# Decode attention with a gated SwiGLU mix: V's loads move from SP's DMA queue to ACT's

## The chip, the cores and the metric

The kernel runs on one core of a Trainium2 chip. The metric is the device time of one execution in microseconds (us); lower is better. "The profile" is one execution recorded by the hardware profiler, with its page and its trace; L187 is line 187 of the kernel before.

## The reference

One new token (batch 1, width 512) goes through two branches, and a sigmoid gate mixes them. Branch A is attention over a cache of 65,536 keys in each of 32 heads, head width 128; branch B is a small SwiGLU.

```python
def _A_ref(x, k_cache, v_cache, wq, wo):          # x: 1 x 1 x 512
    q = (x @ wq).reshape(B, Sq, 32, 128).transpose(0, 2, 1, 3)
    scores = einsum("bhqd,bhkd->bhqk", q, k_cache) * 128 ** -0.5
    p = softmax(scores)                           # 65536 keys in each head
    o = einsum("bhqk,bhkd->bhqd", p, v_cache)
    return o.transpose(0, 2, 1, 3).reshape(B, Sq, 4096) @ wo
def _B_ref(x, w_gate, w_up, w_down):              # 512 -> 1792 -> 512
    return (silu(x @ w_gate) * (x @ w_up)) @ w_down
g = sigmoid((x * gate_w).sum(-1))
return g * A + (1 - g) * B
```

All tensors are bfloat16. The K and V caches are 512 MiB each, and every byte of them is read once.

## The kernel before

It is written in Bass: every engine has an instruction list of its own, and the lists meet only in semaphores. Each head is cut into 8 chunks of 8192 keys (`NCH`, `CK`), so there are 256 K chunks and 256 V chunks (`NT`). A chunk is 2 MiB: 128 partitions with 16 KiB each. In this text k7 is K chunk 7, v7 is V chunk 7, and head h owns chunks 8h to 8h+7 of either kind.

All chunks pass through one ring of 7 buffers (`ring`, `NS`). The order in which they take buffers is `ring_order`: k0 to k9 first, then k10, v0, k11, v1 and so on, V trailing K by `LAG` = 10 chunks, and v246 to v255 at the end. Chunk number n of that list uses buffer n % 7, and its load may start when chunk n-7 has been used. Because 7 is odd and the kinds alternate, the load of a V chunk waits for a K chunk to have been transposed (`ktdone`), and the load of a K chunk waits for a V chunk to have been multiplied (`pvdone`): the load of v(j) waits for the transpose of k(j+7), and that of k(j+14) for the use of v(j). Only among the last ten, where V follows V, is it partly otherwise.

The work on the chunks:

- DVE transposes each K chunk into `kt` (two buffers, L269). After the first chunk of the next head is transposed, it takes the row maximum of the finished head's scores (`mxs`, L275).
- TensorE multiplies the transposed K chunk by the query into `psS` (L346, 64 matmuls), and in the same step the V chunk ten behind by the probabilities into `psO` (L363, 64 matmuls).
- GpSimd reduces the maximum over the partitions (`amx`, L201) and scales it into the bias (`nbias`, L203); later it sums the exponentials (`Lt`, L205).
- ACT does one exponential over the scores of each head (`pa`, L217), as soon as the bias is there. It has hardly anything else to do: two small exponentials at the start (L210, L212), and the store of the output at the end (L220).
- DVE rearranges `pa` into `pb` (L285, 16 copies), which TensorE needs before the head's first V chunk, and normalises a head's result (L290, L292). TensorE adds each head's part of the output product (L372).

SP issues every load, in program order: the two small rows, `wq`, k0 and k1, the three SwiGLU weights, then the chunks in `ring_order`, with `wo` ahead of number 12. Where SP waits for a buffer, all later loads wait behind it.

Of the kernel before, what the change touches and what calls it, by code (L numbers as in the profile page):

```python
# [9 lines left out]
NS = 7  # L10
# [3 lines left out]
ACT = mybir.ActivationFunctionType  # L14
# [8 lines left out]
def bass_gated_mix__mha_block_cached__swiglu_ffn__decode_kernel(  # L23
# [11 lines left out]
    out: bass.AP,  # L35
):
    _, H, S, Dh = A_k_cache.shape
    D = A_wq.shape[0]
    F = B_w_gate.shape[1]
    Dc = D // P  # L40
    FC = F // P
    NCH = S // CK
    NT = H * NCH
    SCALE = float(Dh) ** -0.5
    assert Dh == 128 and D == 512 and F % P == 0 and NCH * RB == 512

    ring_order = []
# [6 lines left out]
    slot = {}  # L54
# [5 lines left out]
    with ExitStack() as ctx:  # L60
        def sb(name, shape, dt):
            return ctx.enter_context(nc.sbuf_tensor(name, shape, dt))

        def psum(name, shape, dt):
            return ctx.enter_context(nc.psum_tensor(name, shape, dt))

        def sem(name):
            return ctx.enter_context(nc.semaphore(name))

        psS = psum("psS", [P, 2, 512], F32)  # L70
# [21 lines left out]
        nbias = sb("nbias", [P, H], F32)  # L92
        rsum = sb("rsum", [P, H], F32)
# [3 lines left out]
        pa = sb("pa", [P, 2, 512], BF16)  # L97
        pb = sb("pb", [P, 2, 512], BF16)
        ring = sb("ring", [P, NS, RB * Dh], BF16)
# [5 lines left out]
        rs = [sem(f"rs{i}") for i in range(NS)]  # L105
# [16 lines left out]
        ktdone = sem("ktdone")  # L122
        qkdone = sem("qkdone")
        pvdone = sem("pvdone")
        s_mx = sem("s_mx")
        s_ar = sem("s_ar")
        s_nb = sem("s_nb")
        expdone = sem("expdone")
        s_pb = sem("s_pb")
# [15 lines left out]
        def kv_src(kind, j):  # L145
            src = A_k_cache if kind == "k" else A_v_cache
            h, c = j // NCH, j % NCH
            return src[0, h, c * CK:(c + 1) * CK, :].rearrange("(p r) d -> p (r d)", p=P)
# [18 lines left out]
        MLP_AT = 2  # L167
        WO_AT = 12

        @block.sync  # L170
        def _(sp):
            sp.dma_start(xrow[0:1, :], xr_dram).then_inc(s_x, 16)
            sp.dma_start(gwrow[0:1, :], gw_dram).then_inc(s_x, 16)
            sp.dma_start(wq_t[:], wq_dram).then_inc(s_wq, 16)
            for n, (kind, j) in enumerate(ring_order):
                if n == MLP_AT:
                    sp.dma_start(wg_t[:], wg_dram).then_inc(s_w1, 16)
                    sp.dma_start(wu_t[:], wu_dram).then_inc(s_w1, 16)  # L178
                    sp.dma_start(wd_t[:], wd_dram).then_inc(s_w1, 16)  # L179
                if n == WO_AT:  # L180
                    sp.wait_ge(s_b, 1)
                    sp.dma_start(wo_t[:], wo_dram).then_inc(s_wo, 16)
                if n >= NS:
                    pkind, pj = ring_order[n - NS]
                    sp.wait_ge(ktdone if pkind == "k" else pvdone, pj + 1)
                sl = slot[(kind, j)]
                sp.dma_start(ring[:, sl, :], kv_src(kind, j)).then_inc(rs[sl], 16)  # L187

        @block.gpsimd
        def _(pool):  # L190
# [16 lines left out]
        @block.scalar  # L207
        def _(act):
            act.wait_ge(s_z, 1)
            nc.scalar.activation(sc[0:1, 1:2], sc[0:1, 0:1], ACT.Exp, scale=-1.0).then_inc(s_e1, 1)  # L210
            act.wait_ge(s_h, 1)
            nc.scalar.activation(hbuf[:, 0, 0:FC], psM[:, 64:64 + FC], ACT.Exp, scale=-1.0).then_inc(s_sig, 1)  # L212
            for h in range(H):
                act.wait_ge(s_nb, h + 1)
                if h >= 2:
                    act.wait_ge(s_pb, h - 1)
                nc.scalar.activation(pa[:, h % 2, :], psS[:, h % 2, :], ACT.Exp, bias=nbias[:, h:h + 1],  # L217
                                     scale=SCALE, accum_out=rsum[:, h:h + 1]).then_inc(expdone, 1)
            act.wait_ge(s_fin, 1)
            act.dma_start(out_dram, fin[0:1, :]).then_inc(s_out, 16)  # L220
            act.wait_ge(s_out, 16)
# [182 lines left out]
```

## Time and profile before

| | |
|---|---|
| median of 3 runs | 2604.34 us (2604.3 to 2604.63) |
| the profiled execution: its own time | 2604.43 us |
| the profiled execution: its span | 2602.6 us |
| busy: DVE, TensorE matmul, ACT, GpSimd | 1324.6, 946.4, 26.6, 34.7 us |
| HBM read | 1087.64 MB, 418 GB/s over the span |
| granted TensorE clock | 1.0 at first, 0.5 from the second of 40 slices on |

The span runs from the first to the last instruction recorded on the core; 1.8 us of the profiled execution's time lie outside it. "DMA" is the mean busy share of the core's 16 DMA engines, which carry the packets of all queues. q1 is the queue of SP, q10 that of ACT, q8 fetches instructions. "SPq" and "ACTq" rows are DMA instructions issued by these engines. Idle time is put down to what ended it.

### The profile page before, as it was taken

The numbers are of one execution on the slowest core, as the hardware profiler recorded it, in microseconds if no ns is written. First come the engines' busy times: TensorE is split into PE (matmuls) and PEld (weight loads), VectorE is DVE, ScalarE is ACT, GpSimd is POOL, SyncE is SP. The second block draws the span as 40 slices with busy tenths as digits, with TensorE's granted clock in tenths as the row PEclk, the third lists the DMA queues.
The fourth block names the chain that finished last, engine by engine and source line by source line (L and its number), as shares of the span: only waits on it lengthen the run. The fifth ranks groups of instructions, "written<-read, shape, count | busy, mean of one in ns | idle before, by whom it ended". The sixth has DMA issues, their size and how long they took to land.

```text
span 2602.6 us, 68273 instructions
## 1 busy us (share of the span) xinstructions
PE 946.4 (36%) x33062; PEld 906.0 (35%) x33062; DVE 1324.6 (51%) x883; ACT 26.6 (1%) x67; POOL 34.7 (1%) x105
## 2 busy tenths in 40 slices
PE   2333333333333333333333333333333333333334
PEld 2333333333333333333333333333333333333333
DVE  4655454554455554555545555455555454554451
ACT  0000000000000000000000000000000000000000
POOL 0000000000000000000000000000000000000000
PEclk9555555555555555555555555555555555555555
DMA  9999999999999999999999999999999999999997
GB/s 397 412 426 426 426 425 426 426 426 427 425 426 426 425 425 427 425 423 419 426 421 423 420 421 423 425 421 420 421 420 425 422 420 425 415 426 423 420 420 309
DMA packets 81512, 1092.03 MB, mean 420 GB/s; under 512 B 8275, under 2 KB 14166, under 8 KB 15190
## 3 DMA queue, kind: packets, MB, share of 16 engines
q1 hardware_dynamic: 81236, 1087.67, 99.1%
q8 instruction: 258, 4.23, 0.7%
q14 instruction: 16, 0.13, 0.0%
q10 hardware_dynamic: 2, 0.00, 0.0%
HBM read 1087.64 MB, written 0.00 MB: 418 GB/s over the span
## 4 chain that ended last, share of the span: by engine, by line
DMA 76%; DVE 12%; PE 9%; issue 1%; SPq 1%; ACT 0%; POOL 0%; POOLq 0%; DVEq 0%
DMA ring<-in_A_k_cache_dram 75%; DVE kt L269 11%; PE psS L346 5%; PE psO L363 4%; DMA ring<-in_A_v_cache_dram 1%; SPq L179 1%; SPq L187 0%; DVE pb L285 0%; PE psB L331 0%; PE psM L324 0%; SPq L178 0%; ACT pa L217 0%; DVE mxs L275 0%; DVE brow L260 0%; POOL amx L201 0%
## 5 line engine op out<-in xcount | busy, mean ns | idle before, releaser
L269 DVE STREAM_TRANSPOSE kt<-ring 128x4096 uint32<-128x4096 uint32 x256 | 1137.5, 4445 | 1142.6 <-DMA ring<-in_A_k_cache_dram 1141.5
L346 PE MATMUL psS<-qd,kt 128*128 128x4 bf16 x16384 | 478.2, 166 | 1606.3 <-DVE kt L269 1606.3
L346 PEld LDWEIGHTS psS<-qd,kt 128*128 128x128 bf16 x16384 | 457.0, 104 | 1640.6 <-DVE kt L269 1640.6
L363 PE MATMUL psO<-pb,ring 128*128 128x1 bf16 x16384 | 472.8, 165 | 30.8 <-DMA ring<-in_A_v_cache_dram 22.7
L363 PEld LDWEIGHTS psO<-pb,ring 128*128 128x128 bf16 x16384 | 456.8, 104 | 32.2 <-DMA ring<-in_A_v_cache_dram 23.8
L285 DVE COPY pb<-pa 32x128 bf16<-32x128 bf16 x512 | 154.5, 302 | 71.3 <-ACT pa L217 64.7
L217 ACT ACTIVATE pa<-psS,nbias 128x512 bf16<-128x512 f32 x32 | 22.0, 687 | 2475.1 <-POOL nbias L203 2475.1
L201 POOL PARTITION_ALL_REDUCE amx<-mxs x32 | 11.8, 368 | 1945.2 <-DVE mxs L275 1945.2
L292 DVE TENSOR_SCALAR oTn<-psO,Li 128x1 bf16<-128x1 f32 x32 | 7.1, 222 | 30.1 <-PE psO L363 29.1
L275 DVE TENSOR_REDUCE mxs<-psS 128x1 f32<-128x512 f32 x32 | 20.9, 653 | 2.0 <-PE psS L346 2.0
L372 PE MATMUL psY<-wo_t,oTn 128*1 128x512 bf16 x32 | 18.8, 587 | 0.4 <-DVE oTn L292 0.4
L205 POOL PARTITION_ALL_REDUCE Lt<-rsum x32 | 12.8, 400 | 285.6 <-issue 285.6
L203 POOL TENSOR_SCALAR nbias<-amx 128x1 f32<-128x1 f32 x32 | 8.3, 260 | 294.4 <-issue 294.4
L310 PE MATMUL psM<-xTb,wq_t 128*128 128x1 bf16 x128 | 3.5, 165 | 11.5 <-DMA wq_t<-in_A_wq_dram 11.5
L310 PEld LDWEIGHTS psM<-xTb,wq_t 128*128 128x128 bf16 x128 | 3.5, 104 | 11.6 <-issue 11.6
L245 DVE CAST qTb<-psM 128x32 bf16<-128x32 f32 x1 | 0.2, 192 | 14.0 <-PE psM L310 14.0
L217 ACT ACTIVATION_READ_ACCUMULATOR pa<-psS,nbias 128x1 f32 x32 | 6.2, 193 | 0.0
L290 DVE RECIPROCAL Li<-Lt 128x1 f32<-128x1 f32 x32 | 4.0, 123 | 3.9 <-POOL Lt L205 3.9
L331 PE MATMUL psB<-wd_t,guT 128*1 128x512 bf16 x14 | 5.9, 613 | 0.0
L260 DVE TENSOR_SCALAR brow<-psB,sc 1x512 f32<-1x512 f32 x1 | 0.7, 737 | 6.5 <-PE psB L331 6.5
L324 PE MATMUL psM<-xTb,wu_t 128*128 128x1 bf16 x56 | 3.2, 165 | 2.1 <-issue 2.1
L324 PEld LDWEIGHTS psM<-xTb,wu_t 128*128 128x128 bf16 x56 | 2.7, 104 | 2.1 <-issue 2.1
(31 smaller groups left out, 19.3 us busy)
## 6 DMA issues: line engine op xcount, KB each, us to landing
ring<-in_A_k_cache_dram SPq DMA_DIRECT2D x256, 2048.0 KB, 31.2
ring<-in_A_v_cache_dram SPq DMA_DIRECT2D x256, 2048.0 KB, 29.9
wq_t<-in_A_wq_dram SPq DMA_DIRECT2D x1, 4096.0 KB, 12.7
wo_t<-in_A_wo_dram SPq DMA_DIRECT2D x1, 4096.0 KB, 32.0
wg_t<-in_B_w_gate_dram SPq DMA_DIRECT2D x1, 1792.0 KB, 26.5
wu_t<-in_B_w_up_dram SPq DMA_DIRECT2D x1, 1792.0 KB, 30.3
wd_t<-in_B_w_down_dram SPq DMA_DIRECT2D x1, 1792.0 KB, 33.8
xrow<-in_A_x_dram SPq DMA_DIRECT2D x1, 1.0 KB
```

The source lines that it names most:

```text
L179: sp.dma_start(wd_t[:], wd_dram).then_inc(s_w1, 16)
L201: nc.gpsimd.partition_all_reduce(amx[:, h:h + 1], mxs[:, h:h + 1], P, RMAX).then_inc(s_ar, 1)
L203: nc.gpsimd.tensor_scalar_mul(nbias[:, h:h + 1], amx[:, h:h + 1], -SCALE).then_inc(s_nb, 1)
L205: nc.gpsimd.partition_all_reduce(Lt[:, h:h + 1], rsum[:, h:h + 1], P, RADD).then_inc(s_L, 1)
L217: nc.scalar.activation(pa[:, h % 2, :], psS[:, h % 2, :], ACT.Exp, bias=nbias[:, h:h + 1], scale=SCALE, accum_out=rsum[:, h:h + 1]).then_i ...
L269: nc.vector.transpose(o, src).then_inc(ktdone, 1)
L275: nc.vector.reduce_max(mxs[:, h:h + 1], psS[:, h % 2, :], AX_X).then_inc(s_mx, 1)
L285: last = nc.vector.tensor_copy(dst, sr)
L292: nc.vector.tensor_scalar(oTn[:, h:h + 1], psO[:, h % 2, h:h + 1], Li[:, h:h + 1], None, ALU.mult).then_inc(s_otn, 1)
L346: last = nc.tensor.matmul(psS[:, h % 2, col:col + 4], ktb[i % 2][:, je // 2, r, :, je % 2], qd[:, h, je, :], start=(je == 0), stop=(je == 3))
L363: last = nc.tensor.matmul(psO[:, h % 2, h:h + 1], ring[:, slot[("v", v)], r * Dh:(r + 1) * Dh], pb[:, h % 2, c * RB + r:c * RB + r + 1], s ...
L372: last = nc.tensor.matmul(psY[0:1, :], oTn[:, h:h + 1], wo_t[:, h, :], start=(h == 0), stop=(h == H - 1))
```

## The change

V's loads are taken out of SP's list and put into ACT's. SP keeps everything else: the small rows, all weights, and K's loads. The conditions on which a load may start, the buffers and `ring_order` stay as they are; a new helper `load` holds the wait and the DMA for both engines.

On ACT the loads stand in program order with the exponentials: the load of v(8h), then the exponential of head h with its waits (`s_nb`, `s_pb`), then the loads of v(8h+1) to v(8h+8), then the exponential of head h+1. All of them stand behind the SwiGLU's exponential (L212 before). ACT's DMA instructions go to ACT's own queue.

```diff
+        def load(eng, n):
+            kind, j = ring_order[n]
+            if n >= NS:
+                pkind, pj = ring_order[n - NS]
+                eng.wait_ge(ktdone if pkind == "k" else pvdone, pj + 1)
+            sl = slot[(kind, j)]
+            eng.dma_start(ring[:, sl, :], kv_src(kind, j)).then_inc(rs[sl], 16)
+
         @block.sync
         def _(sp):
...
-                if n >= NS:
-                    pkind, pj = ring_order[n - NS]
-                    sp.wait_ge(ktdone if pkind == "k" else pvdone, pj + 1)
-                sl = slot[(kind, j)]
-                sp.dma_start(ring[:, sl, :], kv_src(kind, j)).then_inc(rs[sl], 16)
+                if kind == "k":
+                    load(sp, n)
...
-            for h in range(H):
-                act.wait_ge(s_nb, h + 1)
-                if h >= 2:
-                    act.wait_ge(s_pb, h - 1)
-                nc.scalar.activation(pa[:, h % 2, :], psS[:, h % 2, :], ACT.Exp, bias=nbias[:, h:h + 1],
-                                     scale=SCALE, accum_out=rsum[:, h:h + 1]).then_inc(expdone, 1)
+            for n, (kind, j) in enumerate(ring_order):
+                if kind != "v":
+                    continue
+                load(act, n)
+                if j % NCH == 0:
+                    h = j // NCH
+                    act.wait_ge(s_nb, h + 1)
+                    if h >= 2:
+                        act.wait_ge(s_pb, h - 1)
+                    nc.scalar.activation(pa[:, h % 2, :], psS[:, h % 2, :], ACT.Exp, bias=nbias[:, h:h + 1],
+                                         scale=SCALE, accum_out=rsum[:, h:h + 1]).then_inc(expdone, 1)
```

## Prediction, made before the change was run

> **What bounds the kernel now.** I read the page's slices and queues first, then the issues, then the timeline in the middle and at the end.
>
> ```profile
> DMA  9999999999999999999999999999999999999997
> GB/s 397 412 426 426 426 425 426 426 426 427 425 426 426 425 425 427 425 423 419 426 421 423 420 421 423 425 421 420 421 420 425 422 420 425 415 426 423 420 420 309
> ...
> q1 hardware_dynamic: 81236, 1087.67, 99.1%
> q8 instruction: 258, 4.23, 0.7%
> ...
> q10 hardware_dynamic: 2, 0.00, 0.0%
> ```
>
> The 16 DMA engines are busy from the second slice to the last but one, at about 426 GB/s for the first 1100 us and about 421 afterwards. All of it is SP's queue, q1. No engine is near its limit (DVE has the largest share, 51%). So the time is bytes over rate: 1092 MB at the page's mean of 420 GB/s are 2600 us of a 2602.6 us span. The bytes do not change. The time can change only if DMA engines stand idle, or if they move bytes at another rate.
>
> ```profile
> ring<-in_A_k_cache_dram SPq DMA_DIRECT2D x256, 2048.0 KB, 31.2
> ring<-in_A_v_cache_dram SPq DMA_DIRECT2D x256, 2048.0 KB, 29.9
> ```
>
> A load lands some 30 us after its issue. In the timeline K chunks come every 9.8 us (transposes at 1024.37, 1034.15, 1043.94), so one load takes 4.9 us of all engines, and 30 / 4.9 = 6 loads are in the queue at any time. That is the cover that a late issue has.
>
> ```profile
> 1034.15 4.45 DVE L269 STREAM_TRANSPOSE kt<-ring 128x4096 uint32<-128x4096 uint32 x1 [5.34 <-DMA ring<-in_A_k_cache_dram]
> 1038.52 0.65 DVE L275 TENSOR_REDUCE mxs<-psS 128x1 f32<-128x512 f32 x1
> 1038.62 0.33 SPq L187 DMA_DIRECT2D ring<-in_A_v_cache_dram  x1
> ...
> 1039.27 0.37 POOL L201 PARTITION_ALL_REDUCE amx<-mxs  x1 [62.89 <-DVE mxs L275]
> ...
> 1042.26 0.33 SPq L187 DMA_DIRECT2D ring<-in_A_k_cache_dram  x1
> ...
> 1048.42 0.33 SPq L187 DMA_DIRECT2D ring<-in_A_v_cache_dram  x1
> ...
> 1048.56 0.26 POOL L203 TENSOR_SCALAR nbias<-amx 128x1 f32<-128x1 f32 x1 [8.92 <-issue]
> 1048.85 0.69 ACT L217 ACTIVATE pa<-psS,nbias 128x512 bf16<-128x512 f32 x1 [80.17 <-POOL nbias L203]
> ```
>
> This is a head's turn, and the place where the new order of ACT's list bites. The transpose of k(8h+8) frees the buffer for v(8h+1), issued at 1038.62. The same transpose lets DVE take the head's maximum, and the exponential comes only after GpSimd, at 1048.85: between the row of its reduction, 0.37 us, and that of the bias lie 8.92 us.
>
> ```profile
> 2530.55 37.57 SPq L187 DMA_DIRECT2D ring<-in_A_v_cache_dram  x8
> ...
> 2542.22 4.45 DVE L269 STREAM_TRANSPOSE kt<-ring 128x4096 uint32<-128x4096 uint32 x1 [5.35 <-DMA ring<-in_A_k_cache_dram]
> ...
> 2560.02 0.69 ACT L217 ACTIVATE pa<-psS,nbias 128x512 bf16<-128x512 f32 x1 [69.97 <-POOL nbias L203]
> ...
> 2597.43 1.86 PE L363 MATMUL psO<-pb,ring 128*128 128x1 bf16 x64 [3.01 <-DMA ring<-in_A_v_cache_dram]
> ```
>
> The end: k255 lands at 2542.2, its head's exponential runs from 2560.02, the last V chunk lands at 2597.4, and 5 us of small work follow. The V loads of this stretch are issued ahead of that exponential.
>
> **The change, part by part.** *Issuing.* 256 DMA instructions of 0.33 us (84 us) leave SP and come to ACT; ACT's one DMA of before, the output, took 0.50 us, so 84 to 128 us. SP was idle in waits for most of the span, ACT is busy 1%. ACT's exponential of head h stands behind the load of v(8h), which is free once k(8h+7) is transposed, one K period (9.8 us) before the maximum is even taken. Both ends cost nothing: 0 us. That ACT issues on a queue other than SP's shows in q10, the output's.
>
> *K's loads* no longer stand behind V's waits. But they were issued on release already (1042.26 is the end of the V product before it), and 6 queued loads separate issue from service: 0 us.
>
> *Start.* v0 was issued at 58.44; now it stands behind the SwiGLU's exponential, which ran at 60.66 for 0.18 us: 2.4 us late. v1 was issued at 94.49, behind the load of `wo`; now it stands behind head 0's exponential, over at 95.84: 1.4 us late. At 58 us k5 to k10 are queued or landing, and `wo`, issued at 68.22, lands 32.0 us later, at 100.2. Both are covered: 0 us.
>
> *A head's turn.* v(8h+1) was issued at 1038.62; now at the end of the exponential and its accumulator read, 1049.63: 11.0 us late, once in each head. v(8h+2) was issued at 1048.42: 1.5 us late. Queued behind the waiting exponential are these V loads, and TensorE needs v(8h+1) only some 31 us after its old issue. With the two queues served alike, each gets half the rate, 9.8 us for a load. V's queue still holds v(8h) and v(8h-1) when it is cut off, up to 19.6 us of service, so it does not run dry in 11.0 us. If it did, K's queue would take the whole rate. Total bytes in flight fall from 6 loads to 5. Price 0 us; without that cover it would be 31 x 11.0 = 341 us.
>
> *The end.* v249 to v255 stand behind the last exponential. v249 was free when k254 was transposed (2532.43 + 4.45, about 2537); now it goes out after 2560.60, 18.4 us after k255 landed. K's queue is then empty. V's holds v246, v247 and v248: 3 x 4.9 = 14.7 us. If v245 is also still on its way, another 4.9. So the engines stand idle 3.7 us, or not at all. To that comes the way of a fresh load, 1.3 us by the row nearest to it (the gate weights' single row, issued at 1.12 and used at 2.37). Ends 0 and 5.0 us. After that, v249 to v255 queue at once and the end is as before. With two queues abreast v245 is about half done when k255 lands, so I take the middle, 2.5 us.
>
> *The rate with two queues.* Nothing in this trace shows two busy queues for long. The nearest rows are those of q8, which meets q1 some 258 times. By the page q8 had 0.7% of 16 x 2602.6 us for 258 packets, 1.13 us for 16.4 KB; q1 had 99.1% for 1087.67 MB, 0.62 us for as much. In the trace's packet records an instruction packet takes 1.02 to 1.11 us, the next data packet about 1.1, together mostly 2.16 us, where two data packets take 2 x 0.613 = 1.23. So two changes of queue cost 0.94 us, 0.47 each. Those packets go to another place than SBUF and come singly; how much is the change of queue and how much the lone fetch, the rows do not part. Lower end below zero: in the second half the rate is 421.5 where the first had 426; regaining that would be 1460 x 4.5 / 426 = 15 us, and taking away the 16 pairs of changes on each engine (258 / 16 x 0.94) another 15. Upper end: 65,536 data packets over 16 engines are 4096 on each; a change at every one of them costs 4096 x 0.47 = 1925 us. I take 0 us: two queues that are both full have their next packets known in advance, while the instruction fetch comes unannounced.
>
> The Trainium skill's page "DMA: Bandwidth & Descriptors" (Issuing engines are not separate DMA queues) says that all issuers share the same 16 engines and interleave, so a second issuer saves only issue time; by it the rate term is 0. The same page (Queues, rings and completion order) says that an engine drains a whole packet, typically 9 to 17 descriptors, before it goes to another queue. The trace does not show that here: in three of three cases looked at between 1500 and 1530 us, the instruction packet came in after one or two of the eight data packets that a load has on an engine. By the page's rule there would be one change for each load rather than each packet, 512 x 0.47 = 241 us at the full price.
>
> **The sum.** 0 + 0 + 0 + 0 + 2.5 + 0 on the profiled execution's 2604.4 (span 2602.6 and 1.8 outside) is 2606.9; the runs' median, 2604.34, is the same to 0.1 us. Bounds of this case alone: 2604.4 to 2609.4.
>
> **The rivals.**
>
> *Changes of queue cost time (slower).* Place: every data packet on all 16 engines. Price 0.47 us each by q8's rows, so anything up to 4530 us; it decides from 5.2 us / 4096 = 1.3 ns a packet. For it: the only meetings of two queues in the trace all cost. Against it: those are single fetches. At a twentieth of the price, 96 us, the time is 2700.
>
> *V's queue gets more than its half (slower at the end).* If V's chunks are ahead when k255 lands, v248 has landed and nothing is left to move for the 18.4 us until the last exponential is over, plus 1.3: 19.7 us, 2624. For it: the two queues' shares are not bound to be equal. Against: V can not run ahead far, as each V load needs a K transposed.
>
> *Two queues fill small gaps (faster).* The 15 us of the second half come back, up to 30 with the instruction packets: 2574 to 2589. For it: the slower half shows that something stalls. Against: within a packet the engines already run without gaps.
>
> **How the numbers follow.** About 0.2% (5.2 us) is what a measurement of this kernel can tell from no change. The forecast has 0.42 and lies within it; the changes of queue 0.25, more than half of that above 2700; V ahead at the end 0.13; the gaps 0.20. So faster 0.20, same 0.42, slower 0.38. The range goes from 2580 (about 0.05 below, half-way into the gaps' case) to 2700 (about 0.14 above). The forecast's own range is 2604.4 to 2609.4.
>
> **What would show it.** Right: q1 and q10 each with about half of the bytes, slices still at 420 to 426 GB/s, V issues 11 us late once in each head with no idle DMA, and a gap of some 2 us in the DMA near 2557. Wrong: a data packet that takes clearly more than 0.62 us in the queue table (changes of queue), the last exponential later than 2565 with V all landed (V ahead), or slices above 427 (gaps).

## The result

The changed kernel takes 2610.18 us (median of 15 runs, 2607.65 to 2612.28) against 2604.45 us (15 runs, 2604.12 to 2604.98): the ratio is 1.0022, 95% interval 1.0014 to 1.0030. It is 5.7 us slower, and its runs lie 4.6 us apart where those of before lie 0.9 us apart. The profiled execution took 2608.14 us with a span of 2606.3 us, so the trace below shows one of the quicker runs. In the changed kernel ACT's and SP's chunk loads are line 176, the transposes L279, the maximum L285, the head's exponential L227, the V product L373.

From the page: the DMA slices and the queues (packets, MB, share of 16 engines' time).

```profile
DMA  9999999999999999999999999999999999999997
GB/s 397 413 426 425 426 426 425 426 426 426 426 422 419 417 424 425 417 424 418 424 426 420 420 420 419 426 417 426 425 413 426 426 426 417 421 420 426 422 413 318
...
q1 hardware_dynamic: 44372, 550.78, 50.0%
q10 hardware_dynamic: 36866, 536.89, 49.0%
q8 instruction: 258, 4.23, 0.7%
```

V's half of the bytes now runs on q10. 16.4 KB cost 0.620 us on q1 (50.0% of 16 x 2606.3 us for 550.78 MB) and 0.624 us on q10, against 0.622 us when q1 was alone. Two queues that are full at the same time cost the engines nothing that one sees here, although the engines change between them all the time: of 4592 data packets between 200 and 700 us whose follower on the same engine can be told by its start, 3969 were followed by a packet of the other queue. The rate leaves 426 GB/s earlier than before, near the slice of 11 x 65 = 715 us, but then runs about where it ran before.

The issues, with the median time to landing:

```profile
ring<-in_A_k_cache_dram SPq DMA_DIRECT2D x256, 2048.0 KB, 31.4
ring<-in_A_v_cache_dram ACTq DMA_DIRECT2D x256, 2048.0 KB, 25.5
```

V's loads land 4.4 us sooner after their issue than before, K's as before. So V's queue is the shorter one.

A head's turn in the timeline after (start, duration, engine, line, what; an "x2" row is two issues merged):

```profile
1039.95 4.45 DVE L279 STREAM_TRANSPOSE kt<-ring 128x4096 uint32<-128x4096 uint32 x1 [5.35 <-DMA ring<-in_A_k_cache_dram]
1044.32 0.65 DVE L285 TENSOR_REDUCE mxs<-psS 128x1 f32<-128x512 f32 x1
...
1054.93 0.69 ACT L227 ACTIVATE pa<-psS,nbias 128x512 bf16<-128x512 f32 x1 [79.97 <-POOL nbias L208]
1054.93 0.83 ACTq L176 DMA_DIRECT2D ring<-in_A_v_cache_dram  x2
```

The buffer of v(8h+1) is free at 1044.4, when the transpose ends, and its load goes out with the exponential that starts at 1054.93: 10.5 us late. That is the 11 us of the prediction, a little less, as the issue comes with the exponential's start and not after its end.

And the end:

```profile
2547.66 4.45 DVE L279 STREAM_TRANSPOSE kt<-ring 128x4096 uint32<-128x4096 uint32 x1 [5.35 <-DMA ring<-in_A_k_cache_dram]
...
2562.51 0.69 ACT L227 ACTIVATE pa<-psS,nbias 128x512 bf16<-128x512 f32 x1 [68.91 <-POOL nbias L208]
2562.52 0.82 ACTq L176 DMA_DIRECT2D ring<-in_A_v_cache_dram  x2
...
2563.38 7.26 ACTq L176 DMA_DIRECT2D ring<-in_A_v_cache_dram  x5
...
2601.15 1.86 PE L373 MATMUL psO<-pb,ring 128*128 128x1 bf16 x64 [3.02 <-DMA ring<-in_A_v_cache_dram]
```

The seven loads v249 to v255 all go out from 2562.5 on, behind the last exponential. What the DMA engines did meanwhile is in the windows of 5 us (the last two columns are the DMA share and GB/s). First the kernel before:

```profile
2570.00:2575.00 5.00, 2.39 (x65) 1.87 (x65) 0.17 (x1) 0.00 (x0) 0.15 (x1) 0.50 0.96 393
2575.00:2580.00 5.00, 1.87 (x64) 1.79 (x64) 0.00 (x0) 0.00 (x0) 0.00 (x0) 0.50 0.56 233
2580.00:2585.00 5.00, 1.87 (x64) 1.78 (x64) 0.00 (x0) 0.00 (x0) 0.00 (x0) 0.50 0.50 213
...
2590.00:2595.00 5.00, 1.87 (x64) 1.78 (x64) 0.00 (x0) 0.00 (x0) 0.00 (x0) 0.50 0.50 213
```

Then the changed kernel:

```profile
2545.00:2550.00 5.00, 0.94 (x36) 0.85 (x33) 2.34 (x1) 0.00 (x0) 0.00 (x0) 0.50 0.95 400
2550.00:2555.00 5.00, 2.83 (x106) 2.84 (x107) 2.80 (x2) 0.00 (x0) 0.14 (x1) 0.50 0.51 216
2555.00:2560.00 5.00, 3.23 (x122) 3.17 (x120) 0.00 (x0) 0.00 (x0) 0.23 (x1) 0.50 0.50 210
2560.00:2565.00 5.00, 1.06 (x40) 0.97 (x37) 1.61 (x6) 0.78 (x2) 0.26 (x1) 0.50 0.49 125
2565.00:2570.00 5.00, 1.60 (x60) 1.60 (x61) 3.59 (x13) 0.00 (x0) 0.00 (x0) 0.50 0.98 419
...
2585.00:2590.00 5.00, 1.87 (x64) 1.79 (x64) 0.00 (x0) 0.00 (x0) 0.00 (x0) 0.50 1.02 433
```

Before, the share is one half from about 2577 to the end: half of the 16 engines have finished all their packets some 20 us ahead of the other half. The trace also keeps, for every load, the times at which its 16 parts land, one for each engine. Those of v255 fall into eight from 2575.6 to 2576.7 and eight from 2595.5 to 2597.4; they are called its early and its late parts below. The time of the kernel is that of the half that is behind. In the changed kernel the half that is ahead runs dry near 2549 and starts again with the late loads. That costs nothing, as it would have waited later anyway. The half that is behind keeps its 213 GB/s until about 2560; in the window 2560 to 2565 only 125 GB/s were moved, and some of that by the half that had started again, so it stood idle for at least (213 - 125) / 213 x 5 = 2.1 us. The late parts tell the whole: on average those of v248 land at 2562.0 and those of v249 at 2570.0, 8.0 us apart, where before they are 4.9 apart (2561.1 and 2566.0). So 3.1 us were lost here, the start of a fresh load included, and that time is on the path.

### The profile page after: what moved, and what is told of

It reads as the page before. It is cut to its first block, busy times and chain, and to the rows that moved or that the text cites. A ratio compares the mean times of both kernels' runs of the same rounds, so it can differ in the third digit from the quotient of the medians.

```text
span 2606.3 us, 68273 instructions
## 1 busy us (share of the span) xinstructions
PE 944.6 (36%) x33062; PEld 905.3 (35%) x33062; DVE 1325.0 (51%) x883; ACT 26.6 (1%) x67; POOL 34.7 (1%) x105
## 2 busy tenths in 40 slices
DMA packets 81512, 1092.03 MB, mean 419 GB/s; under 512 B 8275, under 2 KB 14166, under 8 KB 15190
## 3 DMA queue, kind: packets, MB, share of 16 engines
q1 hardware_dynamic: 44372, 550.78, 50.0%
## 4 chain that ended last, share of the span: by engine, by line
DMA 78%; DVE 11%; PE 9%; SPq 1%; issue 1%; POOL 0%; ACTq 0%; ACT 0%; POOLq 0%; DVEq 0%
DMA ring<-in_A_k_cache_dram 77%; DVE kt L279 11%; PE psS L356 5%; PE psO L373 4%; DMA ring<-in_A_v_cache_dram 1%; SPq L187 1%; SPq L176 0%; PE psB L341 0%; DVE pb L295 0%; PE psM L334 0%; SPq L186 0%; DVE brow L270 0%; DVE fin L305 0%; DVE mxs L285 0%; SPq L185 0%
## 5 line engine op out<-in xcount | busy, mean ns | idle before, releaser
L279 DVE STREAM_TRANSPOSE kt<-ring 128x4096 uint32<-128x4096 uint32 x256 | 1137.6, 4445 | 1175.6 <-DMA ring<-in_A_k_cache_dram 1174.7
L373 PE MATMUL psO<-pb,ring 128*128 128x1 bf16 x16384 | 472.5, 165 | 28.8 <-DMA ring<-in_A_v_cache_dram 19.2
L373 PEld LDWEIGHTS psO<-pb,ring 128*128 128x128 bf16 x16384 | 456.7, 104 | 30.0 <-DMA ring<-in_A_v_cache_dram 20.1
L227 ACT ACTIVATE pa<-psS,nbias 128x512 bf16<-128x512 f32 x32 | 22.0, 687 | 2477.8 <-POOL nbias L208 2400.4
L285 DVE TENSOR_REDUCE mxs<-psS 128x1 f32<-128x512 f32 x32 | 20.9, 654 | 2.0 <-PE psS L356 2.0
L227 ACT ACTIVATION_READ_ACCUMULATOR pa<-psS,nbias 128x1 f32 x32 | 6.2, 193 | 0.0
```

Of the source, the lines that this page charges most:

```text
L279: nc.vector.transpose(o, src).then_inc(ktdone, 1)
L285: nc.vector.reduce_max(mxs[:, h:h + 1], psS[:, h % 2, :], AX_X).then_inc(s_mx, 1)
L373: last = nc.tensor.matmul(psO[:, h % 2, h:h + 1], ring[:, slot[("v", v)], r * Dh:(r + 1) * Dh], pb[:, h % 2, c * RB + r:c * RB + r + 1], s ...
```

## The experiments

Three theories were put side by side. E: the cost lies at the end, where v249 to v255 wait for the last exponential. M: it lies in the 31 other turns, in each of which a V load is 11 us late. Q: a second queue costs by itself. Ratios are to the kernel before on the same chip, with 95% intervals. These reach about 2.3 us to either side, so a step of 1 to 3 us rests on the runs themselves: on whether those of two kernels overlap, and on what their traces show.

**The last exponential moved out of the way.** Each experiment on ACT's list changes only the V chunk behind whose load a head's exponential stands:

```diff
-                if j % NCH == 0:
-                    h = j // NCH
+                if j in EXP_AT:          # EXP_AT: V chunk -> head
+                    h = EXP_AT[j]
# here: {(NCH * h if h < H - 1 else NT - 2): h for h in range(H)}
```

> V's loads on ACT as in the change; only the last head's exponential moves, from behind the load of v248 to behind that of v254. Theory E (the cost lies at the end: v249 to v255 wait for the last exponential): back to before, 2604 to 2605.5 us, and the runs lie within 1 us of each other again. Theory M (the 31 other turns, in which a V load goes out 11 us late, cost): stays at 2609 to 2611. Theory Q (two queues cost by themselves): stays at 2609 to 2611.

Measured: 2607.66 us (2606.68 to 2608.04), 1.0011 [1.0002, 1.0020]. The runs lie close together again, and 2.5 us are gained, but not all 5.7: the end is part of the cost, and 3.1 us are left (no run overlaps those of the kernel before). None of the three theories alone gives this.

**All other exponentials moved, the last one kept.**

```diff
# EXP_AT = {(NCH * h + 2 if h < H - 1 else NCH * h): h for h in range(H)}
```

> The other half: the exponentials of heads 0 to 30 move behind the load of v(8h+2), so that no V load waits for them; the last head stays as in the change. Theory E: no better than the change, 2607.5 to 2612.5 us. Theory M: 2604 to 2605.5. Theory Q: 2609 to 2611, as E.

Measured: 2609.61 us (2609.23 to 2610.30), 1.0019 [1.0010, 1.0028]. The end by itself costs 5.0 us. Its windows show the same idle time of the half that is behind, longer:

```profile
2555.00:2560.00 5.00, 3.01 (x114) 2.95 (x112) 0.69 (x1) 0.00 (x0) 0.37 (x1) 0.50 0.49 203
2560.00:2565.00 5.00, 2.50 (x94) 2.42 (x91) 0.26 (x1) 0.78 (x2) 0.26 (x1) 0.50 0.17 49
2565.00:2570.00 5.00, 0.18 (x6) 0.18 (x7) 4.73 (x18) 0.00 (x0) 0.00 (x0) 0.50 0.94 344
```

That is (213 - 49) / 213 x 5 = 3.8 us in the middle window alone. By the late parts, v249 lands 10.3 us after v248 (2571.4 and 2561.1), 5.4 more than the 4.9 of the kernel before. The 2.3 us more than in the change have two parts: v248 is in 0.9 us earlier, and the last exponential starts 1.4 us later (2563.93 instead of 2562.51). With no stops in the turns V is further ahead when the last K chunk lands, and less of it is left to bridge that exponential.

**Both moved.**

```diff
# EXP_AT = {(NCH * h + 2 if h < H - 1 else NT - 2): h for h in range(H)}
```

> Both moves together: two queues, and no load waits for an exponential. What is left against before is the second queue alone. Theories E and M: 2604 to 2605.5 us. Theory Q: 2609 to 2611. If two queues fill gaps that one leaves, below 2603.

Measured: 2604.76 us (2604.29 to 2605.29), 1.0001 [0.9992, 1.0010]. The second queue by itself costs nothing and gains nothing, to within the interval; theory Q has fallen. Of the change's 5.4 us over this kernel, freeing the end first takes 2.5 and the turns then 2.9; freeing the turns first takes only 0.6, which lies within the spread of the change's runs, and the end then 4.9. The two parts are not independent.

**More loads held back at the end.**

```diff
# EXP_AT = {(NCH * h if h < H - 1 else NCH * h - 3): h for h in range(H)}
```

> The dose at the end is raised: the last head's exponential stands behind the load of v245, so that v246 to v248 wait for it as well, three loads of 4.9 us more than in the change. Theory E: when k255 has landed only v245 can be left on V's queue, and the engines stand idle for most of the 18.4 us until the exponential is over, plus 1.3 for a fresh load: 15 to 20 us over before, 2619 to 2625 us. Theories M and Q: no more than in the change, 2607.5 to 2613.

Measured: 2625.04 us (2624.25 to 2625.61), 1.0078 [1.0066, 1.0091], at the top of what theory E expected (2619 to 2625). Now all engines stand still:

```profile
2545.00:2550.00 5.00, 3.58 (x128) 3.49 (x128) 0.57 (x1) 0.00 (x0) 0.00 (x0) 0.50 0.29 121
2550.00:2555.00 5.00, 0.20 (x7) 0.21 (x8) 4.45 (x1) 0.00 (x0) 0.00 (x0) 0.50 0.00 0
2555.00:2560.00 5.00, 3.37 (x127) 3.28 (x124) 0.69 (x1) 0.00 (x0) 0.37 (x1) 0.50 0.01 3
2560.00:2565.00 5.00, 0.00 (x0) 0.00 (x0) 0.00 (x0) 0.00 (x0) 0.00 (x0) 0.50 0.00 0
```

Three windows are empty and the ones around them partly so: about 17 of the 20 us can be read off here directly.

**The same waits on one queue.**

```diff
# the kernel before, in SP's loop ahead of the load
+                if kind == "v" and j % NCH == 1:
+                    sp.wait_ge(expdone, j // NCH + 1)
```

> The kernel before, all loads on SP's queue, but SP waits for the exponential of head h ahead of the load of v(8h+1). So the order of the change without its second queue; here K's loads stand behind the wait as well. If the wait by itself costs what it cost with two queues, 2609 to 2611 us. If the six loads in one queue cover 11 us of waiting in every head, and at the end v248 lands (2561.8 in the trace before) after the exponential is over (2560.6), only a fresh load's 1.3 us are lost: 2604.5 to 2606.5. If holding back K too is worse than holding back V, above 2612.

Measured: 2605.53 us (2604.97 to 2606.67), 1.0003 [0.9994, 1.0012]. With one queue the six loads ahead cover the waits; the median is 0.9 us longer, with runs that overlap those of before. So neither the second queue nor the waits cost much alone; the 5.7 us need both.

**How the turns' part adds up.** Four kernels with two queues and the end free differ only in which loads the exponentials of heads 0 to 30 hold back:

```diff
# only head 0:        {(0 if h == 0 else NCH * h + 2 if h < H - 1 else NT - 2): h for h in range(H)}
# heads 16 to 30:     {(NCH * h + 2 if h < 16 else NCH * h if h < H - 1 else NT - 2): h for h in range(H)}
# two loads, 1 to 30: {(0 if h == 0 else NCH * h - 1 if h < H - 1 else NT - 2): h for h in range(H)}
# 1.5 us, 0 to 30:    {(NCH * h + 1 if h < H - 1 else NT - 2): h for h in range(H)}
```

> Two queues; of the 31 turns that cost 3.1 us together when the last head was freed, only head 0's is left: v1 waits for the first exponential, all other exponentials stand behind the loads that they held up. If the turns cost 0.1 us each, 2604.7 to 2605.2 us. If it is the start alone (v1 and v2 go out about 10 us later, while wo is loading), 2607 to 2608.

Measured: 2604.86 us (2604.26 to 2605.15), 1.0001 [0.9992, 1.0010]: the start costs nothing.

> Two queues; only heads 16 to 30 hold back a V load, heads 0 to 15 and the last do not. If the turns cost alike, 15/31 of 2.9 us over the kernel with no turns: 2606.0 to 2606.5. If it is the start alone, 2604.3 to 2605.3. If the cost comes in whenever the loads are held back at any time (it does not add up), 2607 to 2608.

Measured: 2605.69 us (2605.32 to 2607.04), 1.0005 [0.9996, 1.0014]: about 0.9 us over the kernel with no waits in the turns, for 15 turns. That is between nothing and all, and a little less than the even share that was expected; the runs just overlap those of before.

> Two queues, last head freed; in heads 1 to 30 the exponential stands ahead of the load of v(8h), so that v(8h) goes out some 21 us late and v(8h+1) 11 us late in each head. V's queue then has one load left of some 9.8 us at half rate when it is cut off, and runs dry. If a dry V queue leaves the engines to K and costs nothing, 2607 to 2608 us as with one load held back. If each time that V's queue runs dry costs, clearly more: 2609 to 2620.

Measured: 2608.76 us (2604.76 to 2609.85), 1.0012 [1.0003, 1.0021]. Its runs lie 5 us apart, three of the eleven at 2604.8 to 2605.5 and the others at 2607.6 to 2609.9, and the median is only 1.1 us above that with one load held back. Running V's queue lower does not multiply the cost.

> Two queues, last head freed; in heads 0 to 30 the exponential stands behind the load of v(8h+1), so that only v(8h+2) is held back, by some 1.5 us instead of 11 us. If each stop of V's queue costs its 0.1 us whatever its length, 2607 to 2608 us. If the length counts, 2604.5 to 2605.5.

Measured: 2606.24 us (2605.53 to 2607.19), 1.0006 [0.9997, 1.0015]. This lies between the two expectations: waits of 1.5 us cost about half of what waits of 11 us cost. So the part grows with the number of turns and, weakly, with the length of the wait, some 0.1 us a turn.

The landings of the parts show who loses it, and when. Put the late parts of all loads in order of time: those of the kernel with both moved land 2.6 us later than those of the kernel before from the second head to the last but one, an offset that is nearly gone at the end (0.0 to 0.4 us for those of v255). With only the last exponential moved they also land 2.6 us later up to about 750 us, but then slip to 4.1 us by 2450 us, and those of v255 land 1.2 to 3.2 us later than before. So it is the half that is behind that loses the time, and in this trace it loses none of it in the first nine heads. What slows it at a turn is not seen. At a turn the changed kernel's windows do show a dip, 410 and 338 GB/s where it runs at 416 to 426 otherwise:

```profile
1045.00:1050.00 5.00, 3.02 (x114) 2.94 (x111) 0.26 (x1) 0.00 (x0) 0.37 (x1) 0.50 1.01 416
1050.00:1055.00 5.00, 0.76 (x28) 0.77 (x29) 4.18 (x1) 0.07 (x1) 0.26 (x1) 0.50 0.97 410
1055.00:1060.00 5.00, 2.81 (x106) 2.72 (x103) 4.08 (x14) 0.71 (x2) 0.00 (x0) 0.50 0.91 338
1060.00:1065.00 5.00, 0.00 (x0) 0.00 (x0) 4.94 (x4) 0.00 (x0) 0.00 (x0) 0.50 1.00 413
```

But the turn at 1852 of the same trace shows none, and with the turns and the end free the mean rate from 700 to 1000 us falls in the same way as in the change (422 and 421 GB/s, before 426) while the time does not. A share of 0.91 leaves over half of the engines at work, so the dip may lie wholly in the half that is ahead. By what mechanism the turns cost their 3 us stays open.

**An attempt to beat both kernels.** If half of the engines are behind because of the partitions that they write, spreading both halves of the partitions over all engines should bring them level:

```diff
# the kernel before, with buffer semaphores counted in 32
-                sp.dma_start(ring[:, sl, :], kv_src(kind, j)).then_inc(rs[sl], 16)
+                src = kv_src(kind, j)
+                sp.dma_start(ring[0:64, sl, :], src[0:64, :]).then_inc(rs[sl], 16)
+                sp.dma_start(ring[64:128, sl, :], src[64:128, :]).then_inc(rs[sl], 16)
```

> The kernel before with one queue, but every chunk is loaded by two DMAs, partitions 0 to 63 and 64 to 127, on the same buffer semaphore. In the traces half of the 16 DMA engines is done with everything some 20 us before the other half, and from 1100 us on the rate is 421 GB/s instead of 426. If the slower half is slow by the partitions that it writes, and an engine now gets rows of both halves, all engines go alike: the end has no stretch at half share, and the time is 10 to 25 us shorter, 2579 to 2594 us. If the slowness belongs to the engines, 2604 to 2608, with the stretch as before.

Measured: 4672 us, the median of six runs from 4588 to 4724. The ratio to the kernel before, 1.77 [1.767, 1.781], is that of the three quickest (4588 to 4641 us). The page of one that took 4703 us:

```profile
DMA packets 89708, 1092.10 MB, mean 232 GB/s; under 512 B 16467, under 2 KB 22358, under 8 KB 23382
...
q1 hardware_dynamic: 89428, 1087.70, 99.4%
```

The engines are as busy as before and move little more than half. There are 8192 more packets under 512 B than before (16467 and 8275), 16 for each of the 512 additional loads: every load of 64 partitions still ran on 16 engines, but not at full rate. Neither expectation held.

Why half of the engines are behind, this run does not tell, but the traces do: the instruction fetches (q8) fall on that half alone. Towards the end of ten of the traces, twelve fetches start while eight engines move data and the other eight have nothing to do; each time one of the eight at work took the fetch and seven went on with data, though eight others stood idle. The amount fits as well. In the trace before, 96 fetches fall between 195 and 1153 us; a fetch takes 2.16 - 0.61 = 1.55 us from the loads, that is 96 x 1.55 / 8 = 18.6 us for each of eight engines, and in this stretch the distance between early and late parts of K's loads grows from 2.6 to 20.7 us. The half that is ahead meanwhile takes 9.80 us for a K and a V chunk, 16 packets of 0.612 us on each engine, which leaves no room for a fetch. From then on it stays at 21 us, and the rate falls from 426 to 421 GB/s: a buffer is free only when all 16 parts have landed and been used, so the half that is ahead now goes at the pace of the other.

## Why the prediction was right, and where not

The direction of the sum and the mechanism at the end held; the median lies 0.8 us above the forecast's own bounds, 2604.4 to 2609.4, because one term, the head's turn, was set to nothing. That the wide range, 2580 to 2700, holds the result says little: its ends came from two rivals, and neither happened.

- *Issuing, K's loads:* 0 us, and the kernel with all exponentials out of the way confirms it: 0.2 us over before, within the noise.
- *Start:* 0 us; leaving only head 0's wait changes the time by 0.1 us.
- *The rate with two queues:* 0 us was taken from between -30 and 1925, against the nearest rows. The queue table (0.620 and 0.624 us) and the same kernel confirm it. The changes of queue did take place, at nearly every packet, and were free; so the 0.47 us that such a change seemed to cost belongs to the lone fetch of instructions, and is no price of two full queues. That full queues are cheap because their next packets are known in advance is not shown by any run. The rival built on the price is refuted, and so is the one of filled gaps: what the rate loses after 1100 us is no gap that a second queue could fill, but the half of the engines that carries the fetches setting the pace. The fetches are not 16 on each engine, as that rival's price has it, but about 32 on each of eight.
- The Trainium skill's page "DMA: Bandwidth & Descriptors" (Issuing engines are not separate DMA queues), which says that a second issuer saves only issue time, agrees with the 1.0001 of both moved.
- *The end:* 2.5 us, bounds 0 and 5.0. Freeing the end of the change gains 2.5 us, and its trace shows 3.1 us lost there; with the turns free the end costs 4.9, at the upper bound. So that the middle of the bounds came out is in part luck. The gap comes near 2562, not near 2557. What decides its size is how far V is ahead when k255 lands: the rival of V ahead named the right quantity, and its 19.7 us for V wholly ahead is close to what the raised dose measured, 20.5. The working counted 16 engines as one; in fact half of them run dry 12 us earlier, at no cost.
- *A head's turn:* 0 us was wrong; this is the term that was mis-sized. Freeing the turns gains 2.9 us when the end is free and 0.6 us when it is not, and the half of the engines that is behind loses it, from about the ninth head on. The cover by V's queued loads hides all but 1% of the 341 us that the waits would cost without it, and 1% is here half of the result.

## What to carry to other kernels

When a kernel is bound by DMA bytes and its queue is several loads deep, moving loads to a second queue need not change anything by itself (here 1.0001); the price is in what stands ahead of them in the new engine's list. Look at the last occurrence first: in the middle of the run a late load is nearly covered by those queued ahead of it (31 waits of 11 us cost 2.9 us), at the end nothing behind it makes up the time. A wait that must be in such a list belongs behind the loads that are free before it is over: that move alone brought the two-queue kernel back from 2610.2 to 2604.8 us. And where some DMA engines end early, look at what else the others carry: here it was the instruction fetches.

## What the runs showed of the hardware

- Half of the 16 DMA engines finished 20 us before the other half in a kernel of 2604 us, and only the half that was behind set the time; a DMA share of 0.50 over a stretch is how this looks in the windows.
- All twelve instruction fetches that started in such a stretch, in ten traces, went to the busy half, never to one of the idle engines; 258 fetches at 1.55 us on eight engines would be 50 us for each of them (an estimate).
- Two full queues alternated on an engine at nearly every 16 KB packet (3969 of 4592), at 0.620 and 0.624 us a packet against 0.622 with one queue.
- Loads of 64 partitions instead of 128, two on one queue for each chunk and with the same rows of 16 KB, ran at 232 GB/s instead of 420, with the engines 99.4% busy.
- An instruction fetch of 16 KB takes an engine from the loads for about 1.55 us (2.16 us with the next data packet, where that alone takes 0.61), and can come in between the packets of one load.
